# V in eight tiles of its own tokens, key blocks assembled by transfers, loads from two queues

## The chip, the cores and the metric

The kernel runs on one core of one Trainium2 chip. Five engines work in parallel, each through its own list of instructions in order: TensorE (PE, matrix products into PSUM), VectorE (DVE), ScalarE (ACT, table functions such as exp and silu, and copies), GpSimd (POOL) and SyncE (SP, which here only issues transfers). Transfers run on 16 DMA engines; SP and ACT can both issue them. The metric is the device time of one execution in microseconds (us); it is 171.44 us before the change, the median of 3 runs (171.24 to 171.64).

## What is computed

One transformer layer with modulation, on x of 2048 tokens by 448 channels, bfloat16. Attention has 16 heads of 28 channels; each token looks at 8 keys: itself and the 7 at distances 2, 4, ... 14 before it. So even and odd tokens never mix.

```
mod = (silu(c) @ w_mod).reshape(1, 6, 1, -1)
sa, ca, ga, sb, cb, gb = mod[:, 0..5]
h = layernorm(x) * (1 + ca) + sa
q, k, v = split(h @ wqkv)
idx = pos[:, None] - arange(8) * 2                  # masked where negative
attn = softmax(where(idx >= 0, q . k[idx] * 28**-0.5, -1e9))
x = x + ga * ((attn . v[idx]) @ wo)
h = layernorm(x) * (1 + cb) + sb
x = x + gb * (silu(h @ w1) @ w2)
```

## The kernel before, in words

**Tokens and chunks.** The 2048 tokens are cut into NC = 4 chunks of 512, each as CP = 256 even and 256 odd tokens, so that each parity is a sequence of 1024. Chunk 0 comes in two halves, called x0a and x0b. For each chunk `norm1` computes the layer norm: statistics on DVE (`stat`, L470 and L471) or ACT (`total`, `square`, L474 and L480), the power on POOL (L487), the scaling into a tile `xn` (L499 or L501). Then the tile is turned so that channels lie on partitions: on PE for chunk 0 (`on_pe`, L529, modulated by L536 or L538), by a DMA transpose from SP for the others (`on_dma`, L550, modulated in place by L555 or L557). The result is the tile h1, of which three buffers exist; the third lies over the wqk weights.

**Projections.** `project` makes four groups of Q/K products per part (`QK`, L627), cast into the tile `qk` by ACT or DVE (L630). The weights are first padded from 28 to 32 columns per head (`pad`, L564 and L566) out of three loads: the big wqk load of 448 KB, the small wqk block of 224 KB, and wqk3, the rows that are left. V is then computed once per key block (`V`, L638, cast at L642). A key block b holds 128 positions of each parity, from position 112 b on, and serves 112 queries (128 for block 0); nine blocks, NB = 9, cover 1024 positions. Neighbouring blocks overlap by 16 positions, and a block reaches back into the chunk before by 32 k positions for chunk k: each h1 tile therefore has 128 columns of room ahead of its own (HW = 128 + CP), and a halo copy (L611) brings the columns over.

**Attention.** For block b and parity, the logits (`L`, L670) go to PSUM with keys on partitions; ACT takes exp of both halves (L678); DVE multiplies by a mask (L704); `AV` (L730) multiplies by V, whose 29th column of ones gives the sums; DVE divides (L735 and L736, "block output"); a DMA transpose (L740) puts the result into oT. `WO` (L753) projects it with the gated weights, DVE adds to x (L768).

**Feed forward.** Per chunk again a norm (its transposes also at L550), seven products `F1.k.i` (L791), silu on ACT (L794), products `F2` (L808, for the last two tiles L832), the addition (L823 or L838) and the store. The gates ga and gb are multiplied into wo (L879) and w2 (L884); copies of wo are laid at other partitions by two transfers (L882 and L883).

**PSUM.** There are four tiles `ps` of two banks each, called banks in the prediction; logits take two of them at a time. A product waits for a free one, that is, for the cast, exp or addition that reads it.

**Order.** The class `Plan` collects all operations with their dependences and buffers. For the fast layer the string ORDER lists the numbers of the operations in the order in which they are emitted; "v" or "a" behind a number puts an operation that may run on two engines on DVE or ACT. Each engine runs its operations in that order. Exp and silu need different tables on ACT, and a table load (L321) is emitted wherever the kind changes. Transfers are issued through `sp` and `load` (issue at L368). Each transfer takes one of eight landing semaphores in turn (DMAHW0 to DMAHW7), so the ninth waits until the first has landed. A second copy of the layer, with `safe` set, stands behind a branch and runs only if a sum of exps is out of range.

Of the kernel before, what the change touches and what calls it, by code (L numbers as in the profile page):

```python
# [11 lines left out]
ACTF = mybir.ActivationFunctionType  # L12
# [3 lines left out]
D = 448  # L16
# [19 lines left out]
HW = 128 + CP  # L36
# [73 lines left out]


def dram(ap, row, col, dims):

    w = ap.ap[0][0]
    return bass.AP(ap.tensor, ap.offset + row * w + col, [[r * w + c, n] for r, c, n in dims])


class Plan:

    LAT = dict(pe=205.0, act=165.0, dve=125.0, pool=90.0, dma=1500.0, none=0.0, sp=1000.0)
# [119 lines left out]
def layer(ctx, tc, io, safe):  # L242
# [75 lines left out]
    for r, n in (("ps", NPS), ("v", NV), ("p", NP), ("xn", NX), ("o", NB2), ("out", NO), ("dma", 8)):  # L318
        P.resource(r, n)
# [679 lines left out]
```

## Time and profile before

| | |
|---|---|
| median of 3 runs | 171.44 us (171.24 to 171.64) |
| the profiled execution | 171.64 us |
| its span, first to last instruction | 169.9 us |
| clock granted to PE | 0.989 of full |
| bytes moved by DMA | 17.51 MB, mean 103 GB/s |

In the profile a row of a group of instructions reads: line, engine, operation, output <- input, shape, count | busy time in all, mean ns of one | idle time ahead of it and what ended it. Rows of a timeline or of the chain of waits begin with the start and the duration in us. Idle time of an engine that is not the bound costs nothing.

### The profile page before, as it was taken

Reading aid. Unit: us, or ns where it says so; the run is one execution under the profiler, and the core shown is the slowest. Engines: PE = TensorE matmul, PEld = TensorE weight load, DVE = VectorE, ACT = ScalarE, POOL = GpSimd, SP = SyncE. Lnnn points to the kernel's source line nnn. Section 1 sums busy time; section 2 is a strip of 40 time slices with the busy share of each in tenths; the row PEclk is TensorE's granted clock in tenths of the full one; section 3 lists DMA queues with packets and bytes.
Section 4 is the critical chain, followed back from the end, with each engine's and each line's share of the span. In section 5 each row is a group of like instructions: output and inputs, shape, how many; then the busy total and the mean of one; then the engine's idle time right before and its main releaser. Section 6 shows DMA issues by size and latency. Waiting matters only on the chain.

```text
span 169.9 us, 4812 instructions
## 1 busy us (share of the span) xinstructions
PE 162.0 (95%) x2015; PEld 83.9 (49%) x2015; DVE 96.1 (57%) x189; ACT 114.5 (67%) x163; POOL 33.2 (20%) x88
## 2 busy tenths in 40 slices
PE   7799999899999999999999999999999999999990
PEld 2258644545554564455644544655544444445450
DVE  4777999899979963895352577732473000000451
ACT  3148999999876889999878998662767862420000
POOL 7342424730502221132000205120150000000000
PEclk9959999999999999999999999999999999999999
DMA  4994448489979874022020030086008000000031
GB/s 142 289 326 165 99 94 314 78 202 242 176 185 252 177 198 106 0 66 46 20 54 0 4 90 22 2 112 178 6 10 224 0 4 0 0 4 0 38 136 64
DMA packets 32054, 17.51 MB, mean 103 GB/s; under 512 B 23896, under 2 KB 31640, under 8 KB 32024
## 3 DMA queue, kind: packets, MB, share of 16 engines
q1 hardware_dynamic: 31872, 16.90, 39.9%
q8 instruction: 17, 0.28, 0.7%
q10 hardware_dynamic: 152, 0.23, 0.5%
q14 instruction: 13, 0.11, 0.2%
HBM read 9.12 MB, written 1.84 MB: 64 GB/s over the span
## 4 chain that ended last, share of the span: by engine, by line
PE 75%; ACT 10%; DMA 6%; issue 3%; DVE 2%; POOL 1%; ACTq 0%; POOLq 0%
PE ps L791 25%; PE ps L808 22%; PE ps L627 7%; PE ps L753 6%; PE ps L638 5%; ACT p L678 4%; PE ps L730 4%; DMA wqk<-in_A_wqkv_dram 3%; PE ps L832 3%; PE ps L670 3%; DMA x_all<-in_A_x_dram 2%; ACT h L536 2%; ACT qk L630 1%; POOL rs L487 1%; ACT both L480 1%
## 5 line engine op out<-in xcount | busy, mean ns | idle before, releaser
L791 PE MATMUL ps<-h,w 64*128 64x512 bf16 x392 | 44.7, 376 | 0.0
L808 PE MATMUL ps<-w,both 64*128 64x448 bf16 x392 | 39.9, 349 | 0.0
L794 ACT ACTIVATE both<-ps 128x1024 bf16<-128x1024 f32 x28 | 27.3, 1023 | 13.9 <-PE ps L791 13.8
L678 ACT ACTIVATE p<-ps 128x896 bf16<-128x896 f32 (+1 forms) x36 | 31.5, 928 | 3.3 <-PE ps L670 3.2
L791 PEld LDWEIGHTS <-w 64*128 64x128 bf16 x392 | 19.5, 94 | 21.6
L808 PEld LDWEIGHTS <-both 64*128 64x128 bf16 x392 | 18.9, 94 | 17.7
L823 DVE TENSOR_TENSOR ot<-ps,x_all 128x896 bf16<-128x896 f32 x7 | 7.6, 1088 | 34.6 <-PE ps L808 34.3
L627 PE MATMUL ps<-h,wp 64*128 64x256 bf16 (+1 forms) x224 | 20.4, 323 | 0.6 <-ACT h L536 0.4
L627 PEld LDWEIGHTS <-wp 64*128 64x128 bf16 x280 | 13.9, 94 | 11.3 <-issue 1.1
L704 DVE TENSOR_TENSOR p<-p,maskb 128x1792 bf16<-128x1792 bf16 (+1 forms) x18 | 19.3, 1098 | 0.0
L768 DVE SCALAR_TENSOR_TENSOR x_all<-ps,x_all 128x448 bf16<-128x448 f32 x16 | 9.3, 618 | 9.7 <-PE ps L753 9.7
L487 POOL TENSOR_TENSOR rs<-rs,negh 128x2 f32<-128x2 f32 x16 | 13.8, 861 | 1.3
L753 PE MATMUL ps<-wo,oT 64*128 64x448 bf16 x112 | 13.0, 350 | 0.0
L480 ACT ACTIVATE wqk<-x_all,mv 128x448 bf16<-128x448 bf16 x16 | 10.7, 667 | 3.2 <-POOL mv L477 3.0
L477 POOL TENSOR_SCALAR mv<-sums 128x2 f32<-128x2 f32 x10 | 4.8, 479 | 40.0 <-DVE x_all L768 22.2
L638 PE MATMUL ps<-wv,h 64*128 64x448 bf16 x98 | 11.3, 350 | 0.2
L557 DVE TENSOR_SCALAR h<-h,modc 128x512 bf16<-128x512 bf16 x19 | 6.8, 408 | 6.6 <-DMA h<-xn 6.6
L630 ACT CAST qk<-ps 128x1024 bf16<-128x1024 f32 (+1 forms) x12 | 10.0, 871 | 0.7 <-PE ps L627 0.7
L321 ACT ACT_TABLE_LOAD x8 | 10.3, 1283 | 0.1
L486 POOL TENSOR_SCALAR rs<-mv 128x2 f32<-128x2 f32 x10 | 3.6, 356 | 33.3 <-ACT wqk L480 14.5
L736 DVE TENSOR_TENSOR o<-ps,rc 112x896 bf16<-112x896 f32 (+1 forms) x9 | 9.8, 1091 | 0.4
L501 DVE TENSOR_SCALAR xn<-x_all,mv,rs 128x512 bf16<-128x512 bf16 x23 | 8.8, 406 | 1.7 <-POOL rs L487 1.7
(84 smaller groups left out, 161.8 us busy)
## 6 DMA issues: line engine op xcount, KB each, us to landing
out_dram<-ot SPq DMA_DIRECT2D x7, 224.0 KB, 2.2
both<-in_w_mod_dram SPq DMA_DIRECT2D x2, 672.0 KB, 6.0
x_all<-in_A_x_dram SPq DMA_DIRECT2D x3, 448.0 KB, 7.0
w<-in_B_w_dram SPq DMA_DIRECT2D x3, 448.0 KB, 4.2
w<-in_B_w_dram SPq DMA_DIRECT2D x1, 896.0 KB, 5.3
both<-in_w_mod_dram SPq DMA_DIRECT2D x2, 336.0 KB, 5.8
w<-in_B_w_dram SPq DMA_DIRECT2D x1, 672.0 KB, 5.4
wqk<-in_A_wqkv_dram SPq DMA_DIRECT2D x1, 448.0 KB, 5.7
```

The costliest lines, as they stand in the source:

```text
L321: P.load = lambda t: S.preload_act_table(ACTF.Exp if t == "e" else ACTF.Silu)
L480: S.activation(out=scratch[late], in_=x_all[:, us[j], :], func=ACTF.Square, bias=mv[:, j, 0:1], accum_out=mv[:, j, 1:2])
L487: G.tensor_tensor(out=rs[:, j:j + n], in0=rs[:, j:j + n], in1=negh[:, 0:n], op=ALU.pow)
L627: return T.matmul(ps[:, j, 0:2 * n], lhsT=w.rearrange("p h d -> p (h d)"), rhs=h[rows, :, t, c0:c0 + n], start=start, stop=stop)
L630: copy_on(o)(out=qk[:, :, g, :, s0:s0 + n], in_=ps[:, :, 0:2 * n].rearrange("p j (t s) -> p j t s", t=2))
L638: return T.matmul(ps[:, j, 0:D], lhsT=h[rows, j, t, b0:b0 + 128], rhs=wv[rows, t, :], start=start, stop=stop)
L678: S.activation(out=out_, in_=ps[:, :, 0:4 * nq].rearrange("p j (g q) -> p j g q", q=nq), func=ACTF.Exp, scale=SCALE)
L704: V.tensor_tensor(out=p, in0=p, in1=maskb[:, 1 if b == 0 else 0, 0:nq].unsqueeze(1).to_broadcast([128, H, nq]), op=ALU.mult)
L753: return T.matmul(box["ps"][:, j, 0:D], lhsT=oT[rows, j, kk, s0:s0 + 128], rhs=wo[rows, j, kk, :], start=start, stop=stop)
L791: return T.matmul(ps[:, j, :], lhsT=w, rhs=h[rows, :, t, :], start=start, stop=stop)
L794: S.activation(out=hid[:, k % 2, :, i, :], in_=ps[:], func=ACTF.Silu)
L808: return T.matmul(box["ps"][:, par, 0:D], lhsT=hid[rows, k % 2, f % 2, f // 2, 128 * (2 * i + par):128 * (2 * i + par) + 128], rhs=w2[rows ...
```

## The change

V is computed in eight tiles of 128 own positions per parity (two per chunk), cast into three buffers `va`. The key blocks 0 and 8 coincide with the tiles 0 and 7. For each of the seven blocks between, two transfers copy partitions of two neighbouring tiles into a buffer `vb`, 16 b rows from the end of one and 128 - 16 b rows from the start of the other. The room of 128 columns in h1 and the halo copies are gone. Transfers can be issued by SP or ACT, as the order table says. The first w_mod load is ACT's first transfer; x0b is loaded behind the wqk weights; c comes through SP. The two loads of 64 rows each that filled wqk3, and those that filled w13, are merged to one load each, whose source is described as two blocks of 64 rows. `screp` moved into the tile `both`. The order table is a new one throughout (44 lines, of which the rows below show what matters).

```diff
-HW = 128 + CP
...
+def pairs_of(ap, r0, c0, r1, c1, n):
+    w = ap.ap[0][0]
+    return bass.AP(ap.tensor, ap.offset + r0 * w + c0, [[(r1 - r0) * w + c1 - c0, 2], [w, 64], [1, n]])
...
-    NV, NP, NX, NO, NH, NB2 = (4, 5, 2, 2, 3, 2) if not safe else (3, 3, 2, 1, 3, 1)
+    NA, NV, NP, NX, NO, NH, NB2 = (3, 3, 5, 2, 2, 3, 2) if not safe else (3, 3, 3, 2, 1, 3, 1)
...
-    h1 = [ct([128, 2, KT, HW], f"h1_{i}") for i in range(2)] + [wqk_t[:].rearrange("p (t k s) -> p t k s", t=2, k=KT)]
+    h1 = [ct([128, 2, KT, CP], f"h1_{i}") for i in range(2)] + [wqk_t[:, 0:2 * KT * CP].rearrange("p (t k s) -> p t k s", t=2, k=KT)]
...
+    va = [ct([128, 2, H, 32], f"va{i}") for i in range(NA)]
...
+    EITHER = ("sp", "act") if not safe else ("sp",)
+
+    def queue(o):
+        return nc.scalar if o["eng"] == "act" else nc.sync
...
-    ld_x = [[load(224, **first_x(0), run=1792, name="x0a"), load(224, **first_x(1), run=1792, q=nc.scalar, name="x0b")]]
+    ld_x = [[load(224, **first_x(0), run=1792, q=("sp",), name="x0a")]]
...
-    ld_ma = load_mod(0, 2 * D, [first])
+    ld_ma = load_mod(0, 2 * D, [], ("act",))
+    tab = P.op(("act", 1290.0), lambda o: S.preload_act_table(ACTF.Silu), [ld_ma[1]["deps"][0]], name="table")
...
-    ld_qk = [[a], [b], [a], [load(56, wqk3[half(a), 0:D], A_wqkv[128 * (a + 1):128 * (a + 1) + K3, D * (1 - a):D * (2 - a)], late, name="wqk") for a in range(2)]]
+    ld_qk = [[a], [b], [a], [load(112, wqk3[:], pairs_of(A_wqkv, 128, D, 256, 0, D), late, name="wqk")]]
...
+    ld_x[0].append(load(224, after=[x["deps"][0] for x in [ld_qk[0][0], ld_qk[1][0], ld_qk[3][0]]], **first_x(1), run=1792, name="x0b"))
...
-    ld_1 += [load(112, w13[half(a), :], B_w1[128 * (a + 1):128 * (a + 1) + K3, F // 2 * (1 - a):F // 2 * (2 - a)], late, run=1792, name="w1") for a in range(2)]
+    ld_1.append(load(224, w13[:], pairs_of(B_w1, 128, F // 2, 256, 0, F // 2), late, run=1792, name="w1"))
...
-        halo[k] = P.op(either(60.0 + 0.83 * 8 * w, 60.0 + 0.26 * 8 * w), lambda o: copy_on(o)(out=h[:, :, :, 128 - w:128].rearrange("p t k s -> p (t k) s"),
...
+        for t in (2 * k, 2 * k + 1):
+            def make(ps, j, kk, rows, kt, start, stop, t=t):
+                return T.matmul(ps[:, j, 0:D], lhsT=h[rows, j, kt, 128 * (t % 2):128 * (t % 2) + 128], rhs=wv[rows, kt, :], start=start, stop=stop)
...
         for b in BLOCKS[k]:
-            def make(ps, j, kk, rows, t, start, stop, b=b):
-                b0 = 128 + 112 * b - CP * k
-                return T.matmul(ps[:, j, 0:D], lhsT=h[rows, j, t, b0:b0 + 128], rhs=wv[rows, t, :], start=start, stop=stop)
...
+            if b in (0, NB - 1):
+                t = b and 7
+                v_of[b], v_take[b], v_done[b] = (lambda t=t: va_of[t]), (va_take[t], "va"), [va_done[t]]
+                continue
+
+            def shifted(o, b, up):
+                r = 16 * b
+                to, way = (slice(r, 128), slice(0, 128 - r)) if up else (slice(0, r), slice(128 - r, 128))
+                queue(o).dma_start(out=v_of[b]()[to], in_=va_of[b - 1 + int(up)][way])
...
-                nc.sync.dma_start(out=out_view[u // 4, u // 2 % 2], in_=box["o"][:].rearrange("p t d -> p (t d)"))
+                queue(o).dma_start(out=out_view[u // 4, u // 2 % 2], in_=box["o"][:].rearrange("p t d -> p (t d)"))
```

How the new order moves instructions is shown at three places. In these rows L380 is the issue of a load, L669 a copy of V rows into a key block, L564 the transpose of a norm, L769 that of a block output, L571 a modulation, L733 a mask, L515 a norm, L764 and L765 a block output, L799 the addition to x.

ACT at the start of the program before; `both` holds w_mod, c and other small things, `wqk` the big load and the small block, `wp` the padded weights:

```order
L368 DMA x_all<-in_A_x_dram 128x896
L368 DMA both<-in_c_dram 3x128
L368 DMA both<-in_c_dram 1x128
L382 ACT_TABLE_LOAD
L418 ACTIVATE both<-both 4x128
L420 CAST scT<-ps_67 128x4
L564 COPY wp<-wqk 128x32x28
```

The same place after the change, with the semaphores that each instruction waits for; DMAHW0 is taken first by the w_mod load of the first row, DMAHW1 by x0a:

```order
L380 DMA both<-in_w_mod_dram 128x3x896
L380 DMA both<-in_w_mod_dram 64x896
L400 ACT_TABLE_LOAD
L432 ACTIVATE both<-both 4x128 [waits DMAHW3_49,DMAHW2_49]
L380 DMA wqk<-in_A_wqkv_dram 128x2x448 [waits DMAHW0_49]
L380 DMA x_all<-in_A_x_dram 128x896 [waits DMAHW1_49]
L434 CAST scT<-ps_67 128x4 [waits PE_49]
L380 DMA wo<-in_A_wo_dram 64x448 [waits DMAHW5_49]
L578 COPY wp<-wqk 128x32x28 [waits DMAHW4_49]
L380 DMA wv<-in_A_wqkv_dram 128x2x448 [waits DMAHW6_49]
```

x0b and c left the head of ACT's list; w_mod took it, and the small wqk block and x0b follow behind the silu of c.

DVE from the output of block 1 to the second pair of norms of chunk 3, after the change (in the program before, the modulation of chunk 2, four instructions on the tile `wqk`, follows the gating of wo):

```order
L764 RECIPROCAL rc<-ps_69 112x32
L765 TENSOR_TENSOR o_101<-ps_69,rc 112x2x448
L571 TENSOR_SCALAR wqk<-wqk,modc 128x2x256 x4
L733 TENSOR_TENSOR p_99<-p_99,maskb 128x1792
L799 SCALAR_TENSOR_TENSOR x_all,sums<-ps_66,x_all 128x448 x2
L733 TENSOR_TENSOR p_95<-p_95,maskb 128x1792
L733 TENSOR_TENSOR p_96<-p_96,maskb 128x1792
L515 TENSOR_SCALAR xn_81<-x_all,mv,rs 128x512 x2
L764 RECIPROCAL rc<-ps_66 112x32
L765 TENSOR_TENSOR o_100<-ps_66,rc 112x2x448
L733 TENSOR_TENSOR p_97<-p_97,maskb 128x1792
L515 TENSOR_SCALAR xn_81<-x_all,mv,rs 128x512 x2
```

The modulation of chunk 2 moved behind the output of block 1, and the second pair of chunk 3's norms behind the last mask of block 3.

SP from the second transpose of chunk 3 on, after the change; `w_79` is w13, `w_78` the rest of w1, `v_92` the buffer of key block 4:

```order
L564 DMA_TRANSPOSE h_0_83<-xn_81 128x8x128
L380 DMA w_79<-in_B_w_dram 128x1x896
L669 DMA v_92<-va_89 64x1024
L769 DMA_TRANSPOSE oT<-o_101 128x8x112
L380 DMA w_78<-in_B_w_dram 128x1792
L669 DMA v_92<-va_90 64x1024
```

The copies of V rows stand among loads and transposes, which had SP to themselves.

More of the change, by code (lines that the diff above doesn't have):

```diff
@@ L359, in layer, with sp @@
         G.memset(t[:, D:D + 128], 0.0)
-    def sp(ns, fn, deps, land=0.0, give=(), kb=0.0, run=0, eng="sp", name="dma"):
-        a = P.op((eng, ns), fn, deps, take=("dma",), kb=kb, run=run, name=name)
+    def sp(ns, fn, deps, land=0.0, give=(), kb=0.0, run=0, eng=("sp",), name="dma"):
+        a = P.op([(e, ns) for e in eng], fn, deps, take=("dma",), kb=kb, run=run, name=name)
         return P.op(("none", land), none, [a], give=((a, "dma"),) + tuple(give), name=name + "'"), a
+    EITHER = ("sp", "act") if not safe else ("sp",)
+    def queue(o):
+        return nc.scalar if o["eng"] == "act" else nc.sync
     def load(kb, out, in_, after=(), run=896, q=None, name="ld"):
-        q = q or nc.sync
-        return sp(500.0, lambda o: q.dma_start(out=out, in_=in_), list(after), 2300.0 + kb / 0.36, kb=kb, run=run, eng="sp" if q is nc.sync else "act", name=name)[0]
+        return sp(500.0, lambda o: queue(o).dma_start(out=out, in_=in_), list(after), 2300.0 + kb / 0.36, kb=kb, run=run, eng=q or EITHER, name=name)[0]
     def first_x(i):
@@ L590, in duo @@
         return [a, b], e
-    qk_done, v_of, v_take, v_done, qk_mm, v_mm, halo = {}, {}, {}, {}, {}, {}, {}
+    moved = {}
+    qk_done, v_of, v_take, v_done, qk_mm, v_mm, va_of, va_take, va_done = {}, {}, {}, {}, {}, {}, {}, {}, {}
     h1_done, h1_norms = {}, []
@@ L596, in norm1 @@
         h = h1[k % NH]
-        after = [x for kk in (k - NH,) if kk >= 0 for x in qk_mm[kk] + v_mm[kk] + [halo[kk + 1]]] + (pads if k == 2 else [])
+        after = [x for kk in (k - NH,) if kk >= 0 for x in qk_mm[kk] + v_mm[kk]] + (pads if k == 2 else [])
         if k == 0:
@@ new lines, in project @@
+        for b in BLOCKS[k]:
+            if b in (0, NB - 1):
[6 more added lines that the diff above has]
+                queue(o).dma_start(out=v_of[b]()[to], in_=va_of[b - 1 + int(up)][way])
+            (x, a0), (y, a1) = (sp(500.0, lambda o, b=b, up=up: shifted(o, b, up), [va_done[b - 1 + int(up)]], 2000.0, kb=2.0 * (128 - 16 * b if up else 16 * b), run=2048, eng=EITHER, name="vs")
+                                for up in (False, True))
+            a0["take"] += ("v",)
+            P.need(a1, [a0])
+            v_of[b], v_take[b], v_done[b] = (lambda a0=a0: vb[a0["slot"]["v"]]), (a0, "v"), [x, y]
+            moved[b] = [x, y]
+            if b > 1:
+                P.op(("none", 0.0), none, moved[b - 1][1:] + [x], give=((va_take[b - 1], "va"),), name="va free")
@@ L868, in ffn2 @@
             ad = P.op(("dve", 1007.0), lambda o, add=add: add(o), [prev], take=("out",), give=((first, "ps"),), name=f"add{u}")
-            before[:] = [ad, sp(400.0, lambda o, store=store: store(o), [ad], 1400.0, ((ad, "out"),), kb=224.0, run=1792, name=f"st{u}")[1]]
+            before[:] = [ad, sp(400.0, lambda o, store=store: store(o), [ad], 1400.0, ((ad, "out"),), kb=224.0, run=1792, eng=EITHER, name=f"st{u}")[1]]
     for k in range(NC):
```

65 lines of the change are left out of this document (31 added, 34 removed), and 43 rows, old and new, of the table ORDER.

## The prediction

> **What bounds the kernel now.** I read the page first, then the chain of waits, then busy time by stretch, then the timeline and the queue's own waits at the places where the stretches change.
>
> ```profile
> PE 162.0 (95%) x2015; PEld 83.9 (49%) x2015; DVE 96.1 (57%) x189; ACT 114.5 (67%) x163; POOL 33.2 (20%) x88
> ```
>
> TensorE (PE) is busy 95% of the span, so time can come only from less work on PE, an earlier start, or gaps. The chain says where PE is not the bound (start, duration, what):
>
> ```profile
> 0.79 4.17 DMA x_all<-in_A_x_dram
> 4.97 5.66 DMA wqk<-in_A_wqkv_dram
> ...
> 39.13 0.33 PE ps L670 x16
> ...
> 67.64 0.68 ACT L321
> ...
> 124.06 15.97 PE ps L791 x148
> ...
> 150.61 9.84 PE ps L808 x104
> 160.45 0.12 PE ps L919 x2
> 160.57 5.42 PE ps L832 x28
> ```
>
> Loads, then ScalarE (ACT), hold the first 15 us; the rest is PE, with a turn through ACT near 67. The saturated rows give the true pitch of a matmul: 15.97/148 = 108 ns for 512 columns, 9.84/104 = 94.6 ns for 448. By stretch (busy time of PE, PE's weight loads, DVE, ACT, POOL; then PE clock, DMA share, GB/s):
>
> ```profile
> 12.70:36.70 24.00, 22.75 (x373) 13.74 (x376) 21.62 (x45) 23.17 (x39) 10.03 (x20) 1.00 0.57 150
> 36.70:52.30 15.60, 15.60 (x248) 8.22 (x246) 14.22 (x25) 13.96 (x23) 3.31 (x8) 1.00 1.01 218
> ...
> 65.70:72.50 6.80, 6.74 (x92) 3.28 (x90) 4.09 (x7) 6.77 (x8) 1.09 (x3) 1.00 0.20 34
> 72.50:166.00 93.50, 93.47 (x1068) 47.08 (x1062) 35.81 (x64) 56.64 (x74) 10.05 (x20) 1.00 0.19 46
> ```
>
> ACT is full (23.17 of 24.00) until 36.7 while PE looks full too; DMA is full from 36.7 to 52.3; after 72.5 only PE counts. Busy hides slow pitch. I give every matmul group the pitch of its saturated row (groups that never saturate, such as AV's 32 in 0.90, by their rows in the chain) and sum in program order: from the first Q/K product at 12.73 to 160.45 PE needs 142.3 us and takes 147.7. So 5.4 us are lost: 2.8 before the third block's first logits (L3.0) at 39.13, 2.6 behind it, about half of that around 65.7 to 72.5.
>
> **The change part by part.** The order table is new throughout, so I follow what each engine waits for.
>
> *Fewer V tiles.* Nine V blocks become eight.
>
> ```profile
> L638 PE MATMUL ps<-wv,h 64*128 64x448 bf16 x98 | 11.3, 350 | 0.2
> L642 ACT CAST v<-ps 128x896 bf16<-128x896 f32 x4 | 3.6, 909 | 1.2 <-PE ps L638 1.1
> L642 DVE CAST v<-ps 128x896 bf16<-128x896 f32 x5 | 5.4, 1088 | 2.7 <-PE ps L638 2.5 <-ACT p L678 0.2
> L611 ACT COPY wqk<-h 128x512 bf16<-128x512 bf16 x1 | 0.6, 619 | 0.0
> L321 ACT ACT_TABLE_LOAD x8 | 10.3, 1283 | 0.1
> ```
>
> 14 matmuls at 94.6 ns: **-1.3 us**, certain, as PE bounds the last 90 us. One eviction (0.9 to 1.1) and three halo copies (0.6, 0.3, 0.2) leave ACT and DVE, and the new table has six table loads where there were eight. These matter where ACT or DVE leads, below.
>
> *The start.* In both programs eight transfers can be in flight: the ninth waits for the first to land. Before, that held the big wqk load to 4.97:
>
> ```profile
> SPq L368 <- DMA x_all<-in_A_x_dram: 1.3, 1, 1.3
> SPq L368 <- DMA both<-in_w_mod_dram: 0.9, 1, 0.9
> 8.42 0.37 SPq L368 DMA_DIRECT2D x_all<-in_A_x_dram  x1
> L368 SPq DMA_DIRECT2D x_all<-in_A_x_dram x4: 367/400/468, 0.8 to 8.4; - x4
> DMA to landing us min/median/max: 3.9/5.4/7.1
> GB/s 142 289 326 165 99 94 314 78 202 242 176 185 252 177 198 106 0 66 46 20 54 0 4 90 22 2 112 178 6 10 224 0 4 0 0 4 0 38 136 64
> L470 DVE BATCH_NORM_STATS2 st<-x_all 128x6 f32<-128x448 bf16 x12 | 7.3, 606 | 2.1 <-DMA x_all<-in_A_x_dram 2.1
> 14.69 2.91 PE L627 MATMUL ps<-h,wp 64*128 64x256 bf16 x50 [0.36 <-ACT h L536]
> ```
>
> Now the big wqk load goes out from SP among the first eight, near 2.1, but the small wqk block and x0b stand on ACT behind the landing of the 672 KB of w_mod (DMAHW0 in the rows of ACT shown with the change). Before, w_mod landed at 8.4 (x3's issue at 8.42 waited for it). Now it starts a microsecond sooner and shares with x0a and wqk; by the slices' 142 and 289 GB/s, 1344 KB (two equal shares of 672) are through at 6.8. The wqk block then lands 4.2 later (bounds 3.9 and 7.1), 11.0; one pad on DVE (0.39) and first Q/K at 11.7 instead of 12.73. x0b lands near 11.5; behind it on DVE stand four statistics (0.61 and some 0.15 for the aggregation each; two are chunk 1's) and two norms (0.41), then two transposes on PE (0.5), and behind those L0.0: 15.9. The Q/K casts and the table load set the first exp: 11.7 + 3.2 (56 matmuls at 2.91/50 = 58 ns) + 0.8 + 1.28 = 17.0, against
>
> ```profile
> 18.05 1.02 ACT L678 ACTIVATE p<-ps 128x1024 bf16<-128x1024 f32 x1
> 39.80 1.72 ACT L678 ACTIVATE p<-ps 128x896 bf16<-128x896 f32 x2
> 29.50 3.73 ACT L630 CAST qk<-ps 128x1024 bf16<-128x1024 f32 x4
> ```
>
> **-1.0 us** (bounds -1.4, and +1.8 with the slow landing).
>
> *ACT from the first exp to block 3's.* Before, 18.05 to 39.80 without a gap over 0.2. The same stretch after the change has one modulation (0.81) and one V cast (0.91) more, and one Q/K cast (0.93), the halo copy (0.62), one square with its read (0.8) and one sum (0.7) fewer: -1.3. But a modulation of chunk 1 now stands on ACT ahead of block 1's exps and waits for transposes that leave SP only behind x0b's norms: +0.7 (0 to 1.7). **-0.6**; exp 3.0 then starts at 38.2 and L3.0, 0.4 ahead of it, at 37.8, 1.3 early. By then PE has done both gates and the second column products but no part of chunk 2's Q/K: 0.4 us more than before. With the V tile, the work left is 117.1 us against 118.8: at this point the change is **3.0 us ahead**.
>
> *What gives it back.* The three key places are one loop: norm on DVE, transpose from SP, modulation on DVE, product on PE.
>
> ```profile
> 51.27 1.40 DVE L557 TENSOR_SCALAR h<-h,modc 128x512 bf16<-128x512 bf16 x4 [0.98 <-DMA h<-xn]
> 55.44 4.26 SPq L550 DMA_TRANSPOSE h<-xn  x2
> 49.21 1.09 DVE L736 TENSOR_TENSOR o<-ps,rc 112x896 bf16<-112x896 f32 x1
> L550 SPq DMA_TRANSPOSE h<-xn x12: 1231/1232/2176, 18.0 to 128.0; - x12
> DMA to landing us min/median/max: 2.7/2.7/4.5
> wo<-wo SPq DMA_DIRECT2D x1, 224.0 KB, 5.3
> ```
>
> Before, chunk 2's modulations stood behind the gating of wo instead. Now, in the rows of DVE shown with the change, they stand behind block 1's output (0.35 + 1.09), so chunk 2's Q/K waits 1.0. AV2 and AV3 wait for masks queued behind those modulations and the adds: 0.9. Chunk 3's second pair of norms stands behind the last mask of block 3: 0.7 norms, 3 to 3.5 transpose, 1.4 modulations, 0.2 signals, against about 4 us of PE work that can run meanwhile: 1.4. The key blocks cost 14 new transfers, 1.79 MB in 2 KB rows; at 289 GB/s 6.2 us of all engines, most of it in a stretch whose DMA share was 1.01 (one w2 load of 672 KB moves out of it). That lengthens the transposes on the path by 0.5 (0 if there is room, 1.8 each if all land at 4.5). F1.0 now runs as seven products in a row, without the table switch at 67.64; the exps of blocks 5 and 6 follow with at most one bank to spare: 0.8.
>
> On SP, the merged load of w13 stands in front of block 4's copies (the rows of SP shown with the change). Its source is described as two blocks of 64 rows, the destination as 128 rows; no load before has a source whose outer dimension is two. If it runs like the others, 224 KB take 0.8 us; if only two of 16 engines carry it, 5.6 us at the slice's 326 GB/s (41 GB/s for two), and everything behind it on those engines is late. AV4 stands some 8 us of issue and PE work behind it; the chain over the load, one transpose (1.3), a 448 KB load (1.5) and the copies is 5 or 9.8 long. AV4's wait is 0 to 1.8; I take 1.4, as the description differs just in that dimension. Waits behind L3.0: 1.0 + 0.9 + 1.4 + 0.5 + 0.8 + 1.4 = 6.0, against 2.6 before: **+3.4**.
>
> The Trainium skill speaks against these loads: DMA: Bandwidth & Descriptors, "Why a DMA increments its semaphore by 16 and not by 1", says that a transfer uses the largest number of engines up to 16 that divides the slowest dimension of both sides, here two. No run here shows it. With its roughly 27 GiB/s per engine the load would take an estimated 3.9 us.
>
> *The end.* The last product is the same 28 matmuls in 5.42, the add and the last store unchanged: 0.
>
> Sum: -3.0 + 3.4 = +0.4 on the profiled execution's 171.64 (span 169.9 and 1.7 around it): 172.0. That execution lies 0.2 above the median 171.44, so **171.8 us**.
>
> **The rivals.** *The gain is kept.* If the waits behind L3.0 are no longer than the 2.6 of before, the end is 171.44 - 3.0 = 168.4. For it: fewer DVE and ACT instructions, two table loads less. Against it: the loop above has no slack in rows, and DMA was full there.
>
> *Slow merged loads.* Both loads whose source is two blocks crawl on two engines: w13 costs AV4 the full 1.8 (0.4 more), and wqk3 ahead of chunk 1's x delays x0b's statistics and ACT's next issue (both wait for its successors) by about 1: 173.2. It decides if either lands over 7 us behind its issue. This is the skill's rule above at its full price.
>
> *Copies crowd the transposes.* Chunk 2's, chunk 3's and the second norm's transposes each land 4.5 instead of 2.7 behind issue: 3 x 1.8 less the 0.5 counted: 171.8 + 4.9 at most; with half of it hidden 174.2. For it the share of 1.01, against it the moved w2 load and idle DMA before 26.
>
> **How the numbers follow.** Forecast 0.45, gain kept 0.23, slow merged loads 0.24, crowded transposes 0.08. The forecast's own range is 170.7 to 172.9. This kernel's runs tell no change within 0.2% (0.34 us). Of the forecast 0.13 lies under that, 0.12 within, 0.20 above: faster 0.36, same 0.12, slower 0.52. Range 168.4 to 174.2.
>
> **What would show it.** Right: the first Q/K product at 11 to 12.5; first exp near 17; ACT without gaps to block 3; PE gaps before chunk 2's and chunk 3's Q/K and before AV4; V products 112 instead of 126. Wrong: the small wqk block landing after 13 (start lost) or before 10 (slot wait harmless); PE without gaps from 38 to 62 (gain kept); w13 landing within 5 us of issue (no slow load); transposes over 4 us in the median (crowding).

## The result, and the profile after

| | before | changed |
|---|---|---|
| median, us | 171.47 (171.24 to 171.64, 4 runs) | 181.78 (180.70 to 183.34, 4 runs) |
| ratio, 95% interval | 1 | 1.061 (1.051 to 1.071) |
| profiled execution: time, span | 171.64, 169.9 | 182.72, 181.0 |
| first exp | 18.05 | 20.72 |
| L3.0 (first logits of block 3) | 39.07 | 43.44 |
| from L3.0 to the end of the span | 130.8 | 137.6 |

Here and below a median is that of all executions, while a ratio leaves out those more than 1.5% above the fastest of their kernel; the profiles of w13_cols, both_rows, both_rows_again, w13_late and thin are of such executions.

The change is 10.3 us slower; the forecast was 171.8 and the range ended at 174.2. On the profiled execution the forecast stood at 172.0, so 10.7 us are missing: 5.6 at L3.0 (43.44 where 37.8 was forecast) and 5.0 behind it. For the second: before needed 130.8 us from L3.0, of which 2.6 were waits; the change has 1.7 us less to do there, so 130.8 - 2.6 - 1.7 = 126.5 would be no waits at all. It took 137.6, 11.0 us of waits and slow products, where the prediction had 6.0.

The busy row and the clock row of the page of after:

```profile
PE 164.2 (91%) x2001; PEld 83.1 (46%) x2001; DVE 97.2 (54%) x197; ACT 105.2 (58%) x149; POOL 30.6 (17%) x87
PEclk9975999999999985999999999999999999999997
```

PE is busy for longer than before with 14 matmuls fewer, and the clock row has two dents, in the third and fourth slice (9 to 18 us) and in the fifteenth and sixteenth (63 to 72). The chain of waits of after passes through both (start, duration, what):

```profile
1.62 4.27 DMA both<-in_c_dram
...
6.00 6.57 DMA wqk<-in_A_wqkv_dram
12.59 0.41 DVE wp L578
13.04 5.73 PE ps L638 x54
...
23.73 4.54 DMA h<-xn
...
41.08 4.34 DMA wqk<-xn
45.52 1.39 DVE wqk L571 x4
46.96 2.98 PE ps L638 x26
...
60.27 7.64 DMA v<-va
68.05 1.01 PE ps L759 x32
69.06 1.60 PE ps L784 x7
...
171.37 5.42 PE ps L863 x28
```

The small wqk block leaves ACT at 6.00, behind the landing of c, and lands at 12.57. The 54 Q/K products behind it take 106 ns each, where before had 58. Block 4's copies land 7.64 us behind their issue, and after them seven output products take 1.60 us (229 ns each, where the saturated pitch is 94.6). Busy time by stretch, with the granted clock in the third column from the end:

```profile
9.50:11.20 1.70, 0.00 (x0) 0.00 (x0) 0.92 (x3) 0.08 (x1) 0.00 (x0) 1.00 1.07 294
11.20:13.00 1.80, 0.40 (x2) 0.10 (x1) 0.39 (x1) 0.94 (x2) 0.00 (x0) 0.61 0.93 290
13.00:18.00 5.00, 4.96 (x48) 3.51 (x50) 4.05 (x11) 1.17 (x2) 1.36 (x4) 0.50 0.31 98
...
63.66:66.00 2.34, 0.00 (x0) 0.00 (x0) 0.74 (x2) 2.11 (x3) 0.75 (x2) 1.00 1.06 339
66.00:68.00 2.00, 0.00 (x0) 0.00 (x0) 0.00 (x0) 0.00 (x0) 0.00 (x0) 0.56 1.35 103
68.00:73.00 5.00, 4.95 (x54) 2.54 (x56) 1.45 (x2) 0.81 (x1) 0.00 (x0) 0.50 0.56 125
73.00:74.00 1.00, 1.00 (x14) 0.43 (x12) 0.62 (x1) 0.00 (x0) 0.00 (x0) 0.98 0.67 99
```

Both times PE stands idle first, then works at half the clock for 5 us, and "busy" hides it. Here an idle PE is thus paid twice.

### The profile page after: what moved, and what is told of

Same layout as the page of the kernel before. It is cut to its first block, busy times and chain, and to the rows that moved or that the text cites. A ratio compares the mean times of both kernels' runs of the same rounds, so it can differ in the third digit from the quotient of the medians.

```text
span 181.0 us, 4798 instructions
## 1 busy us (share of the span) xinstructions
PE 164.2 (91%) x2001; PEld 83.1 (46%) x2001; DVE 97.2 (54%) x197; ACT 105.2 (58%) x149; POOL 30.6 (17%) x87
## 4 chain that ended last, share of the span: by engine, by line
PE 69%; DMA 20%; DVE 6%; issue 1%; ACT 1%; SPq 0%; DVEq 0%; ACTq 0%
PE ps L822 23%; PE ps L839 17%; PE ps L638 12%; PE ps L784 5%; DMA oT<-o 5%; DMA v<-va 4%; DMA wqk<-in_A_wqkv_dram 4%; PE ps L648 3%; PE ps L759 3%; PE ps L863 3%; DMA h<-xn 3%; DMA wqk<-xn 2%; DMA both<-in_c_dram 2%; PE ps L699 2%; DVE h L571 1%
## 5 line engine op out<-in xcount | busy, mean ns | idle before, releaser
L638 PE MATMUL ps<-h,wp 64*128 64x256 bf16 (+1 forms) x224 | 23.9, 364 | 4.6 <-ACT h L550 2.3
L638 PEld LDWEIGHTS <-wp 64*128 64x128 bf16 x280 | 15.3, 105 | 18.5 <-issue 6.2
L733 DVE TENSOR_TENSOR p<-p,maskb 128x1792 bf16<-128x1792 bf16 (+1 forms) x18 | 19.4, 1102 | 1.3 <-ACT p L707 1.3
L515 DVE TENSOR_SCALAR xn<-x_all,mv,rs 128x512 bf16<-128x512 bf16 x32 | 11.9, 407 | 13.3 <-POOL rs L501 13.3
L494 ACT ACTIVATE wqk<-x_all,mv 128x448 bf16<-128x448 bf16 x16 | 10.7, 668 | 11.7 <-POOL mv L491 11.6
L641 ACT CAST qk<-ps 128x1024 bf16<-128x1024 f32 (+1 forms) x15 | 12.7, 870 | 6.1 <-PE ps L638 6.0
L784 PE MATMUL ps<-wo,oT 64*128 64x448 bf16 x112 | 13.9, 366 | 0.5 <-ACT gbc L467 0.2
L569 ACT ACTIVATE h<-h,modc 128x512 bf16<-128x512 bf16 x5 | 4.0, 810 | 17.6 <-DMA h<-xn 17.6
L571 DVE TENSOR_SCALAR h<-h,modc 128x512 bf16<-128x512 bf16 x19 | 6.8, 409 | 12.3 <-DMA h<-xn 12.3
L501 POOL TENSOR_TENSOR rs<-rs,negh 128x2 f32<-128x2 f32 x16 | 11.5, 717 | 1.3
L759 PEld LDWEIGHTS <-p 128*128 128x128 bf16 x288 | 7.8, 97 | 7.1 <-issue 6.1
L759 PE MATMUL ps<-v,p 128*128 128x29 bf16 x224 | 6.8, 177 | 4.4 <-DMA v<-va 4.4
L648 PE MATMUL ps<-wv,h 64*128 64x448 bf16 x84 | 10.6, 367 | 0.1
L799 DVE SCALAR_TENSOR_TENSOR x_all<-ps,x_all 128x448 bf16<-128x448 f32 x16 | 9.3, 621 | 2.2 <-PE ps L784 2.2
```

The costliest lines, as they stand in the source:

```text
L501: G.tensor_tensor(out=rs[:, j:j + n], in0=rs[:, j:j + n], in1=negh[:, 0:n], op=ALU.pow)
L515: V.tensor_scalar(out=out_, in0=in_, scalar1=mv[:, j, 0:1], scalar2=rs[:, j:j + 1], op0=ALU.subtract if b else ALU.add, op1=ALU.mult)
L638: return T.matmul(ps[:, j, 0:2 * n], lhsT=w.rearrange("p h d -> p (h d)"), rhs=h[rows, :, t, c0:c0 + n], start=start, stop=stop)
L641: copy_on(o)(out=qk[:, :, g, :, s0:s0 + n], in_=ps[:, :, 0:2 * n].rearrange("p j (t s) -> p j t s", t=2))
L648: return T.matmul(ps[:, j, 0:D], lhsT=h[rows, j, kt, 128 * (t % 2):128 * (t % 2) + 128], rhs=wv[rows, kt, :], start=start, stop=stop)
L733: V.tensor_tensor(out=p, in0=p, in1=maskb[:, 1 if b == 0 else 0, 0:nq].unsqueeze(1).to_broadcast([128, H, nq]), op=ALU.mult)
```

## The experiments

For all of them I read three numbers from the profiled execution: the first exp, L3.0, and the rest from L3.0 to the end of the span (the span less L3.0). The rest leaves out how the start went. Executions of one kernel differ by up to 4.6 us (w13_cols, 180.50 to 185.11), and the rest of one kernel by 1.4 in two executions (both_rows and both_rows_again), so smaller differences of one profile say little. The runs belong to several sessions; each ratio is to executions of the kernel before in the same session (medians 171.47 to 172.04), and medians of different sessions are compared through these ratios.

| kernel | median, us | ratio to before, 95% | first exp | L3.0 | rest |
|---|---|---|---|---|---|
| before | 171.47 | | 18.05 | 39.07 | 130.8 |
| changed | 181.78 | 1.051 to 1.071 | 20.72 | 43.44 | 137.6 |
| w13_rows | 176.80 | 1.029 to 1.037 | 19.95 | 42.28 | 131.9 |
| w13_cols | 181.72 | 1.052 to 1.061 | 22.35 | 45.14 | 138.3 |
| both_rows | 174.22 | 1.008 to 1.017 | 20.12 | 42.76 | 132.0 |
| before_cols | 171.48 | 0.997 to 1.004 | 17.67 | 38.69 | 131.1 |
| early | 180.13 | 1.041 to 1.059 | 17.98 | 41.01 | 138.0 |
| rows_early | 174.04 | 1.005 to 1.021 | 17.29 | 40.35 | 132.6 |
| rows_fill | 176.52 | 1.025 to 1.039 | 17.98 | 40.17 | 132.2 |
| av4_fill | 180.50 | 1.042 to 1.060 | 21.49 | 44.28 | 134.8 |
| rows_x0b | 173.97 | 1.009 to 1.026 | 17.15 | 39.78 | 132.6 |
| rows_oldstart | 175.29 | 1.017 to 1.031 | 18.41 | 41.32 | 131.9 |
| w13_late | 178.54 | 1.027 to 1.046 | 20.16 | 42.83 | 134.4 |
| rows_x0b_late | 174.97 | 1.015 to 1.028 | 16.72 | 39.55 | 132.1 |
| best | 171.63 | 0.996 to 1.003 | 16.55 | 38.10 | 132.1 |
| both_rows_again | 174.35 | 1.002 to 1.020 | 18.69 | 41.63 | 133.4 |
| thin | 173.06 | 1.000 to 1.008 | 18.24 | 40.67 | 131.9 |
| thick | 172.60 | 1.002 to 1.010 | 17.27 | 39.90 | 132.9 |
| best2 | 172.47 | 1.000 to 1.007 | 18.85 | 40.08 | 132.3 |

### The shape of the merged loads

w13_rows and w13_cols both make two transfers of the one w13 load; `load` issues one per pair. They differ in how it is cut:

```diff
-    ld_1.append(load(224, w13[:], pairs_of(B_w1, 128, F // 2, 256, 0, F // 2), ...
+    # w13_rows
+    ld_1.append(load(224, [w13[half(a), :] for a in range(2)],
+        [B_w1[128 * (a + 1):128 * (a + 1) + K3, F // 2 * (1 - a):F // 2 * (2 - a)] for a in range(2)], ...
+    # w13_cols
+    ld_1.append(load(224, [w13[:, F // 4 * a:F // 4 * (a + 1)] for a in range(2)],
+        [pairs_of(B_w1, 128, F // 2 + F // 4 * a, 256, F // 4 * a, F // 4) for a in range(2)], ...
```

> The changed kernel, its one merged load of w13 split into two loads of 64 rows each, issued one behind the other in the same place. Theory A (the two-block source keeps the load on few engines, and block 4's copies land late behind it): the copies land about 3 us behind their issue instead of 7.6, PE's 4.4 us wait ahead of AV4 falls under 1.5 us, PE's clock there stays at 1.00, and the time falls from 181.8 to 174 - 177 us. Theory B (the copies are late because of where they stand on SP and what they share, whatever the load's shape): the wait stays over 3 us and the time within 1.5 us of 181.8.

> The same split into two loads, but by columns: each half still takes its source as two blocks of 64 rows, so number of transfers, bytes and semaphores are those of the split by rows. Theory A: as slow as the changed kernel, copies over 6 us behind issue, AV4's wait over 3 us, 180 - 183.5 us. Theory B: within 1 us of the split by rows.

Cut by rows 176.80, by columns 181.72, as slow as uncut. PE's row of AV4 in the timeline of the changed kernel, then of w13_rows, and then of w13_cols (the bracket is PE's idle time ahead of it):

```profile
68.05 1.01 PE L759 MATMUL ps<-v,p 128*128 128x29 bf16 x32 [4.39 <-DMA v<-va]
```

```profile
63.29 0.95 PE L759 MATMUL ps<-v,p 128*128 128x29 bf16 x32 [0.63 <-DMA v<-va]
```

```profile
69.20 1.01 PE L759 MATMUL ps<-v,p 128*128 128x29 bf16 x32 [3.77 <-DMA v<-va]
```

Bytes, number of transfers and place are the same; the source's outer dimension of two is left in w13_cols, and with it the wait. (Its rows are half as long as well, but the uncut load, with whole rows, is as slow.) Theory A holds: 5 us in the median, 5.6 in the rest (137.6 against 131.9). Of the 5.6, 3.6 stand between L3.0 and AV4 (24.6 us against 21.0) and 2.0 behind the start of AV4 (113.0 against 110.9). The slow load shows in its successors: in the changed kernel the copies land 7.64 us behind issue, in w13_rows 4.14 (issue 59.02). One sign of theory A failed: in w13_cols they land 4.70 behind their issue, not over 6. There the delay stands ahead of it: the copy and the transpose before them take 2.14 and 2.28 us on SP (0.54 and 1.29 in w13_rows), and the copies leave 19.2 us behind L3.0, where the changed kernel's leave at 16.8.

before_cols puts the same two-block halves into the kernel before, in the place of its two loads by rows.

> The kernel before with one thing changed: its two loads of w13 are cut by columns, each with a source of two blocks of 64 rows, instead of by rows. Theory A: each half takes about 2.5 - 4 us longer to land and what follows it on the same engines is late: 172 - 177 us. Theory B: within 0.5 us of 171.5.

171.48: no cost that the interval shows. Theory A's number for it was wrong, though the shape does slow what follows: the output transpose issued near 50 lands 5.4 us behind its issue, 3.2 in the kernel before. PE shows no wait from 36 to 75. So the shape costs where someone waits for what stands behind it. w13_late moves the merged load behind block 4's copies:

```diff
- 51 52 376 377 421 261 262 265 388 389 47 48 263 264 266 267 270
+ 376 377 421 261 262 265 388 389 47 48 263 264 266 267 270 51 52
```

> The changed kernel, its merged loads as they are, with the load of w13 issued behind block 4's last copies instead of ahead of them. Theory A: the copies land about 4 us behind issue, AV4 waits under 1 us, the late landings move to transposes that are needed only near 75: 175.5 - 177.5 us. Rival J (the two-block load costs its time wherever it stands, by the transposes and copies behind it): 179 us or more.

178.54, between the two theories, with a rest of 134.4 between 131.9 and 137.6. AV4's wait fell to 0.34, but what now stands behind the load on SP is late: two transposes of a norm land 6.2 and 7.1 us behind their issue, and the second keeps SP for 4.01 us. The transpose of block 4's output, ready at 65.96, leaves SP only at 68.55. From the timeline of w13_late:

```profile
71.44 0.93 PE L782 MATMUL ps<-wo,oT 64*128 64x448 bf16 x8 [1.75 <-DMA oT<-o]
```

both_rows also cuts wqk3 by rows; both_rows_again is the same kernel once more.

> Both merged loads (wqk3 and w13) split by rows. Theory A: beyond the split of w13 alone, wqk3 lands about 3 us sooner than its 7.5 us and the small wqk block with it, the first full run of Q/K products starts at 11 - 12 us instead of 13.0, another 1 - 3 us: 172 - 175 us. Rival C (at the start the 1 KB loads of c, landing at 5.9, hold ACT's issue of the small wqk block, and PE's idle time there costs it clock): first Q/K run still at 12.5 - 13.2 us at a granted clock near 0.66, under 0.7 us gained over the split of w13 alone.

> The same kernel as both_rows, for another profiled execution. Theory N (the start of this kernel varies from run to run with the clock that PE is granted after its idle time): median 173.5 - 176; an execution under 174.3 shows a clock over 0.9 from 13 to 17 and its 54 Q/K products in 3.1 - 3.5 us; an execution over 175.5 shows 0.5 - 0.7 and over 4.5 us. Theory O (splitting wqk3 brings the small wqk block in sooner): a fast execution has the block landed by 11.5.

The median falls another 2.6 us, but not because the small block lands sooner. Theory O falls: the block lands at 13.01 in the one profiled execution and holds Q/K until 13.07 in the other. Their rows for the first full run of Q/K products, both_rows and then both_rows_again:

```profile
13.49 4.63 PE L638 MATMUL ps<-h,wp 64*128 64x256 bf16 x54 [2.84 <-DVE wp L578]
```

```profile
13.07 3.16 PE L638 MATMUL ps<-h,wp 64*128 64x256 bf16 x54 [1.65 <-DVE wp L578]
```

The same products took 4.63 us with the clock at 0.50 to 0.69 until 17, and 3.16 with the clock at 1.00, so the start does vary with the clock. Theory N's rule for the total fails, though: the execution with the good start took 176.74, its rest being 1.4 us longer. The profiled ones lie 2.3 and 2.4 us above their medians; what the 172.35 us execution did isn't seen, and how much of the 2.6 us is wqk3's shape stays open here. `early` and rows_early, below, show that shape's cost at another place.

### The start

rows_early and `early` issue the small wqk block from SP, right behind the large one:

```diff
- 57 58 59 15 16 13a 14 21a 22
+ 13 14 57 58 59 15 16 21a 22
```

> Both merged loads split by rows, and the small wqk block (224 KB) issued from SP right behind the large one instead of from ACT behind silu. Theory C (the block is late because its issue stands on ACT behind the landing of c, and PE's idle time there costs it clock): the block lands at 8.5 - 10 instead of 13.0, the first full Q/K run starts at 10.3 - 11.5 at a granted clock of 0.9 - 1.0, the first exp at 15.5 - 17.5 instead of 20.1, 169 - 171.5 us. Rival D (the bytes of the first 12 us decide, 2 MB at about 320 GB/s, whatever the order of issue): first Q/K run not before 12.5, less than 1 us gained on 174.2.

> The changed kernel with the merged loads as they are and the small wqk block issued from SP right behind the large one. Theory C: the first full Q/K run at 10.3 - 12 instead of 13.0 at a clock of 0.9 - 1.0; AV4 still waits over 3 us for block 4's copies; 176 - 179 us. Theory A at the start (the merged wqk3 load, on few engines, holds the blocks behind it): wqk3 still lands 7 us or more behind issue and the first Q/K run starts at 12 or later: 179 us or more.

Theory C is right on the place: with both loads by rows the first full Q/K run starts at 11.44 instead of 13.49, in 3.28 us, and the first exp comes at 17.29. With wqk3 merged the first Q/K product starts at 12.37, held by wqk3's own pad on DVE, which stands ahead of the modulations. The rows of that pad, `early` and then rows_early:

```profile
10.74 0.28 DVE L580 COPY wp<-wqk 128x448 bf16<-128x448 bf16 x1 [2.22 <-DMA wqk<-in_A_wqkv_dram]
```

```profile
9.35 0.28 DVE L580 COPY wp<-wqk 128x448 bf16<-128x448 bf16 x1 [0.33 <-DMA wqk<-in_A_wqkv_dram]
```

So the two-block shape costs 1.4 us here, 0.7 of it at the first exp, and was hidden in the changed kernel behind the later small block. The time missed its range: rows_early's ratio (1.005 to 1.021) is no better than both_rows's (1.008 to 1.017). `early` came out as theory A had it (180.13), and its AV4 still waits 4.62 us. Part of rows_early's earlier exp was lost before L3.0 (23.1 us from first exp to L3.0, 21.0 before).

Two kernels try the clock by itself. rows_fill puts 14 matmuls of the warm-up kind ahead of the first Q/K products; av4_fill puts 18 into the changed kernel's wait ahead of AV4:

```diff
-        junks.append(P.op(("pe", 431.0), lambda o: warm_up(w_last, 2), ...
+        junks.append(P.op(("pe", 431.0), lambda o, n=len(junks): warm_up(w_last, 16 if n == JUNK - 1 else 2), ...
```

```diff
             box["o"] = ob[o["slot"]["o"]]
+            if b == 4:
+                for _ in range(18):
+                    T.matmul(bank(o)[:, 0, 0:D], lhsT=ident[:], rhs=wv[:, 0, :], start=True, stop=True)
```

> Both merged loads split by rows, and 14 more matmuls of the warm-up kind (results unused) on PE ahead of the first Q/K products, so that PE does not stand idle while it waits for the small wqk block. Theory E (idle time lowers the clock that PE is granted, and the products behind it run at half pitch): the clock from 13 to 17 is 0.9 - 1.0 instead of 0.5 - 0.6, the 54 Q/K products take 3.1 - 3.4 us instead of 4.6, the first exp comes 1.2 - 2 us sooner, 172 - 173.2 us. Rival F (those products are slow for another reason, such as loads landing meanwhile): still 4.5 us, 174.2 within 0.5 us.

> The changed kernel with its merged loads as they are, and 18 extra matmuls (results unused) on PE ahead of AV4, into the bank that AV4 then overwrites. Theory E: block 4's copies land as late as before, but PE's clock from 66 to 72 is 0.9 - 1.0 instead of 0.52 and the products behind AV4 run at their usual pitch: 2 - 3 us gained, 178.8 - 179.8 us. Rival F: clock or not, those products are slow for want of something else: 181.8 within 0.7 us.

The stretch from 66 to 72 in av4_fill:

```profile
66.00:72.00 6.00, 6.00 (x77) 3.41 (x77) 2.28 (x3) 1.07 (x2) 0.00 (x0) 1.00 0.73 98
```

The clock stays at 1.00 (0.52 in the changed kernel), though only useless work was added, as theory E has it. Its gain is smaller than the rest suggests. The rest shrinks by 2.7 us, from 137.6 to 134.8, but 1.0 of that stands ahead of AV4, which starts 23.6 us behind L3.0 instead of 24.6; the copies left SP 15.8 behind it instead of 16.8. Behind the start of AV4 the rest is 111.2 instead of 113.0, so the half clock cost some 1.7 us there. The median, 180.50, lies outside the ranges of both theories, and its interval overlaps the changed kernel's, so the median alone shows no gain.

rows_fill kept the clock at 1.00 too, and in its profile, of its fastest execution, the first exp comes 2.1 us ahead of both_rows's, as E expects. But it comes only 0.7 ahead of both_rows_again's, whose clock was 1.00 without a filler, and the ratio of rows_fill (1.025 to 1.039) is worse than both_rows's. A fixed filler costs its time whenever the block lands early; that reason is argued, no trace shows it.

rows_x0b sends x0b among the first eight transfers and the small block right behind it; rows_oldstart goes back to the first loads of the kernel before:

```diff
- 0 1 75 74 76 77 78v 4 5 6 7 2 3 8 9 10 64 11 12 57 58 59 15 16 13a 14 21a 22 65
+ 0 1 75 74 76 77 78v 4 5 6 7 2 3 8 9 10 64 11 12 21 22 13 14 57 58 59 15 16 65
```

```diff
+ 0 1 8v 9 75 74 21a 22 4a 5 2a 3 10 76 77 78v 64 6v 7 57 58 59 15 16 11 12 13 14 65
```

> Both merged loads split by rows, and now x0b from SP among the first eight transfers with the small wqk block behind it, instead of x0b from ACT behind the landing of w_mod. Theory G (x0b's place behind w_mod makes chunk 1's statistics, norms and transposes late, and these hold the stretch from the first exp to block 3): x0b lands by 9 instead of 12.1, chunk 1's transposes land at 22.5 - 24 instead of 25.2, L3.0 stands at 38.3 - 39.5 instead of 40.35, 172 - 173.2 us. Rival H (the work of DVE and ACT fills that stretch whatever x0b does): L3.0 at 40 or later, 174 us within 0.6.

> Both merged loads split by rows, and the first loads in the order of the kernel before: x0b and c from ACT first, all weights from SP behind x0a (the modulation's second), so that the change's order of the first loads is undone and the rest of it kept. Theory G: first exp at 17.5 - 18.5, L3.0 at 38.5 - 39.5, 172 - 173.3 us: weights first gained nothing. Rival I (weights first is a gain that something else hid): first exp after 19, 174.5 us or more.

Neither theory had the size: x0b sooner moved L3.0 from 40.35 to 39.78 and the median not at all. With the old first loads the median is 175.29, as rival I said, though the first exp, at 18.41, is where G put it. That is 1.3 us over rows_x0b in the same session, but the intervals of the two overlap, and some 0.7 of it may be the clock: behind a pause of 1.57 us PE ran from 10.3 to 13.4 at 0.52, and its 56 Q/K products took 3.98 us where 54 take 3.16 in rows_x0b. That the weights of the modulation belong first is thus not shown.

### What remains

rows_x0b_late has the split w13 behind the copies as well.

> The loads of rows_x0b, with the (split) load of w13 behind block 4's copies too. Theories A and G together: AV4's remaining wait of 0.7 us goes as well, 171.3 - 172.6 us, level with the kernel before; if AV4's wait is set by block 4's own V product instead, no better than rows_x0b.

No gain: AV4 waited 1.13 us instead of 0.72, with the copies issued 1.6 us sooner. Another release took the copies' place; the profile names a norm on DVE. thin and thick price the copies' bytes. In both, ACT fills the key tiles once while it waits for c; thin moves one row per transfer and leaves out the others, so that its values of blocks 1 to 7 are not the layer's:

```diff
-                to, way = (slice(r, 128), slice(0, 128 - r)) if up else (slice(0, r), slice(128 - r, 128))
+                to, way = (slice(r, r + 1), slice(0, 1)) if up else (slice(0, 1), slice(128 - r, 129 - r))
```

> rows_x0b with each of the 14 transfers that put the key blocks together cut to one row of 2 KB (so values of blocks 1 to 7 are not the reference's), and the three key tiles filled once by ACT while it waits for c. Theory L (the copies' bytes lengthen the transposes and hold AV4): transposes 0.5 - 1 us faster in the median, AV4's wait under 0.3, at least 0.8 us under thick. Rival M (bytes are hidden; AV4 waits for a bank that ACT frees anyway): within 0.5 us of thick.

> rows_x0b with the same three fills by ACT and the copies whole: the yardstick for thin. All theories: 174.0 within 0.7 us.

173.06 against 172.60, with ratios of 1.000 to 1.008 and 1.002 to 1.010: rival M. The 1.79 MB are hidden, as far as these intervals tell. (thick lies 1.4 under rows_x0b of another session, from which it differs only in these fills; so much two sessions can differ, if the fills do nothing.)

best is rows_x0b with chunk 1's first two norms (162, 163) on DVE and their transpose (170) on SP ahead of x0b's modulations (93, 94), the last norm (169) and the second transpose (172) ahead of the copy for the gates (67), and on PE F1.1's product (560) ahead of WO2.0 (501):

```diff
- 129 93v 94v 95 166 130 330 124 116 331 131a 125 117 167 126 118 120 112 161 121 122 162v 163v 170 171 113 168v 67 169v 172 173 174 127v
+ 129 161 162v 163v 170 171 93v 94v 95 166 130 330 124 116 331 131a 125 117 167 126 118 120 112 121 122 168v 169v 172 173 174 113 67 127v
...
- 486 501 560 622
+ 486 560 501 622
```

> rows_x0b with two places of the order changed: on DVE chunk 1's norms (and on SP its transposes) ahead of x0b's modulations and of the copy for the gates, and on PE the first half of WO2.0 behind one more product of F1.1. Theory K (the new order, not the V tiles, holds the rest): chunk 1's transposes land about 1 us sooner than 24.6, L3.0 at 38.7 - 39.3 instead of 39.78, WO2.0's wait of 0.4 gone, 172.4 - 173.4 us. Rival H (DVE and ACT are full there and only trade places): L3.0 at 39.5 or later, 174 within 0.5.

171.63 us, level with the kernel before (0.996 to 1.003), better than theory K had it, and 1.0 under thick in the same session. ACT's modulation of chunk 1 in rows_x0b and then in best:

```profile
24.70 0.81 ACT L569 ACTIVATE h<-h,modc 128x512 bf16<-128x512 bf16 x1 [1.39 <-DMA h<-xn]
```

```profile
22.80 0.81 ACT L566 ACTIVATE h<-h,modc 128x512 bf16<-128x512 bf16 x1
```

The wait is gone, and L3.0 stands at 38.10, a microsecond ahead of before and 0.3 from the 37.8 of the prediction. What is left of the difference lies behind L3.0 (132.1 against 130.8). best2 goes after two of those waits: block 4's copies ahead of a w1 load on SP, two casts ahead of two squares on ACT, WO3.0 behind one more product.

```diff
- 423 422 403 419v 307 299 308 295 296 424 425 309 300 260a 297 310a 298a
+ 403 419v 307 299 308 295 296 309 300 260a 297 310a 423 422 424 425 298a
...
- 47 48 263 264 266 267 270
+ 263 264 266 267 270 47 48
...
- 612 591 592 629
+ 591 592 612 629
```

> best with three more places of the order changed: block 4's copies ahead of a w1 load on SP, the casts of V5 and of the first Q/K product of chunk 3 ahead of two squares on ACT that wait for POOL, and the first part of WO3.0 behind one more product of F2. Theory K (what is left is order): AV4's wait of 0.94 under 0.4 and WO3.0's of 0.60 gone, 170.4 - 171.2 us, 0.3 to 0.7% under the kernel before. Rival M (another release, a bank or a mask, holds AV4 at the same place, 21 us behind L3.0): AV4's wait stays over 0.7, 171.6 within 0.4 us.

172.47 us, outside the ranges of both theories. The waits ahead of AV4 and WO3.0 are gone, and the one that took their place stands one product on, behind the cast that the squares now hold up:

```profile
62.77 0.74 PE L645 MATMUL ps<-wv,h 64*128 64x448 bf16 x6 [0.83 <-ACT qk L638]
```

The rest is no shorter, 132.3. No kernel here beats the one before beyond its interval.

## Why the prediction was wrong, step by step

**Fewer V tiles, -1.3: stands.** The groups of after count 112 V products where 126 stood. Nothing measured the 1.3 us alone.

**The start, -1.0: wrong, +2.7 at the first exp.** Two steps failed. The step "the wqk block then lands 4.2 later, 11.0" took a time near the lower of its own bounds (3.9 and 7.1); measured are 6.57, from an issue at 6.00 that was even earlier than the 6.8 reckoned, and so 12.57. And the 56 products were priced at 58 ns, as if an idle PE kept its clock: they took 106, which is 2.5 us. rows_early shows that the rest of the reckoning was sound: with the small block on SP the first exp came at 17.29, where 17.0 was forecast.

**ACT from the first exp to block 3's, -0.6: wrong, +1.5.** Busy time and length of this stretch, before and then after (ACT is the fourth busy time):

```profile
18.05:39.80 21.75, 20.86 (x328) 11.01 (x326) 20.64 (x39) 21.50 (x36) 8.75 (x18) 1.00 0.69 173
```

```profile
20.72:43.97 23.25, 21.50 (x362) 12.34 (x357) 20.63 (x40) 20.54 (x31) 4.46 (x13) 1.00 0.65 176
```

ACT's work fell by 1.0 (1.3 forecast); its idle time is 2.7 where the step allowed 0.7. The wait for chunk 1's transposes that the step named is 1.6, just under its upper bound of 1.7; the others are PE's late logits and V product. best shows that the named wait hung on the order on DVE and SP: with x0b already early, norms and transposes ahead of x0b's modulations removed it.

**The waits behind L3.0, 6.0: 11.0.** The term that was mis-sized is AV4's, 1.4 with a cap of 1.8. It was 4.39 us of wait and some 2 us of slow products behind it (113.0 us from the start of AV4, where av4_fill took 111.2 and w13_rows 110.9). The cover was judged well: PE arrived at AV4 7.6 us behind the issue of w13 (56.03 to 63.66), 8 were reckoned. The chain was not: the copies landed 11.9 behind that issue, where 9.8 were reckoned. Of the others, the sum was about right (5.4 in w13_rows less AV4's 0.6 is 4.8, against 4.6 forecast) and the places were not, so that sum is luck. Chunk 2's Q/K waits 0.92 (1.0 forecast), but DVE stood idle 1.32 us for the transposes ahead of those modulations; block 1's output had nothing to do with it. The masks of AV2 and AV3 (0.9) and chunk 3's second norms (1.4) show no gap over 0.25 on PE, the copies' bytes (0.5) cost nothing that thin shows, and the first column products run on without a gap. In w13_rows 3.7 of the 5.4 us lie in no gap over 0.25, and what makes them up stays open.

**The rivals.** "Slow merged loads" was the right mechanism with the right mark ("over 7 us behind its issue": some 7.5 for wqk3, from its issue near 2.6 to its pad at 10.1, which waited for it; w13's own landing is not in the trace, but the copies behind it took 7.64). Its price, 1.4 us over the forecast, was a fraction of the 10 that were missing, since it capped AV4's wait at 1.8 and counted no clock behind the waits; nor did it have the late small block. Its chance of 0.24 was too low for a rule with a mark of its own. Bearing on it: the Trainium skill (DMA: Bandwidth & Descriptors, "Why a DMA increments its semaphore by 16 and not by 1") has the number of engines divide the slowest dimension of both sides; w13_rows against w13_cols agrees, though no view here counts engines. "The gain is kept" and "copies crowd the transposes" fell: transposes land in 2.8 us in the median with whole copies and with thin ones alike. The second one of chunk 2 does take 4.5, as that rival had it, but with thin copies too (4.49, and 4.50 with whole ones).

**What was left out** is the clock. It stood in the profile of before, in a view that I had read for other things (busy time by stretch, before):

```profile
7.00:8.20 1.20, 0.01 (x1) 0.02 (x2) 1.10 (x4) 0.00 (x0) 0.71 (x2) 1.00 1.08 295
8.20:9.30 1.10, 1.10 (x36) 1.06 (x36) 0.46 (x2) 0.00 (x0) 0.89 (x2) 1.00 1.02 289
9.30:12.50 3.20, 3.10 (x21) 1.65 (x17) 2.65 (x11) 1.65 (x3) 1.09 (x3) 0.50 0.99 334
```

PE stands still for 1.2 us, and 1.1 us later works 3.2 us at half the clock. What ran there was mostly transposes and warm-up products, so I take it to have mattered little. The long waits of PE in the prediction should have carried a second price.

## What to carry to other kernels

Before merging two loads, look at the outer dimension of both sides, not at the bytes: one of 224 KB whose source is two blocks cost 5 us, and in the kernel before, where PE did not wait for what stood behind it, nothing, so the test is what the next few entries of the queue are wanted for. Price a gap on PE of over a microsecond twice, as the wait and as a risk of half the clock for the 3 to 7 us that follow (here 2.5 us at the start, some 2 behind AV4, nothing at the start of `early`), and read the granted clock by stretch wherever PE's products look long. A change in structure comes with an order of its own; undo the loads' shapes, the first issues and the order on the norm's engine one by one before blaming or crediting the structure.

## What the runs showed of the hardware that I had not expected

PE's clock can fall after short pauses. Besides the 1.2 us in the kernel before, best2's start shows it (busy time by stretch):

```profile
6.00:8.00 2.00, 1.73 (x39) 1.31 (x39) 0.41 (x1) 0.32 (x2) 0.56 (x3) 1.00 0.98 352
8.00:9.20 1.20, 0.05 (x1) 0.06 (x2) 0.83 (x4) 0.31 (x1) 0.00 (x0) 0.77 0.81 123
9.20:11.60 2.40, 2.04 (x7) 0.90 (x9) 1.58 (x6) 1.17 (x3) 0.00 (x0) 0.50 1.02 326
11.60:15.20 3.60, 3.47 (x32) 2.58 (x33) 2.46 (x8) 0.77 (x3) 0.91 (x2) 0.50 0.96 292
```

A pause of 1.2 us, then half the clock for 6 us though PE was busy for nearly all of it. In rows_x0b a pause of 1.41 us at the same place cost nothing (clock 1.00 from 10 to 17), and in `early` neither did one of 2.67 us (clock 1.00 from 7 to 17). From the timeline of `early`:

```profile
12.37 0.29 PE L638 MATMUL ps<-h,wp 64*128 64x256 bf16 x2 [2.67 <-ACT h L550]
12.83 3.16 PE L638 MATMUL ps<-h,wp 64*128 64x256 bf16 x54 [0.17 <-ACT h L550]
```

What else decides is not seen here. The Trainium skill (TensorE: Matmul & The Clock Gate, "HAM oscillation — how this bites in real kernels") warns of pauses over about 3.4 us; these traces show the drop after 1.2, and not each time. Slower executions of one kernel often show a lower mean clock: the changed kernel's spans of 179.0, 179.1, 181.0 and 181.6 us come with 0.981, 0.966, 0.956 and 0.956. It is not the only cause: two executions of rows_fill took 176.90 and 177.55 us at a mean clock of 1.00, its fastest 174.10 at 0.997.
